# Second mixture layer of a gated model: when the second tile's rows are gathered, and which of ScalarE's and VectorE's work is issued first

## The chip, the cores and the metric

The kernel runs on one core of one Trainium2 chip. TensorE (PE) does the matrix products, ScalarE (ACT) and VectorE (DVE) take results out of PSUM and convert weights, GpSimd (POOL) issues the gathers and scatters of rows, SyncE (SP) issues the loads of weights. The metric is the device time of one execution in microseconds (us), the median of three runs.

## The reference

Attention is followed by two mixture-of-experts layers over 2304 tokens with 512 features and 8 experts of 1024 hidden units. The change lies in the second of them:

```python
def _moe2_ref(x, w_skip, w_gate, w1, w2) -> np.ndarray:
    N, D = x.shape
    E = w_gate.shape[1]
    skip_score = x @ w_skip
    do_compute = skip_score > 0
    out = x.copy()
...
    xc = x[do_compute]
    logits = xc @ w_gate
    e_idx = np.argmax(logits, axis=1)
...
    for e in range(E):
        mask = e_idx == e
        if not mask.any():
            continue
        h = np.maximum(xc[mask] @ w1[e], 0.0)
        y[mask] = gate_w[mask, None] * (h @ w2[e])
    out[do_compute] = xc + y
    return out.astype(np.float32)
```

## The kernel before

The second layer goes through the eight experts one after the other, in places 0 to 7. An expert's tokens are known only when the first layer is done, so they are taken in tiles of 128 rows. The first tile of a place is always computed, by straight code that this document calls region 0 to region 7. A second and a third tile stand behind run-time branches (`tc.If`, L1449 to L1468): `ffn2s` for a second tile of at most 64 rows, `ffn2` for a larger one. In this run place 0 has three tiles, places 2 and 5 a small second one, place 6 a large second one; places 1, 3, 4 and 7 have one tile. Every place issues the gather of a second tile, whether it has rows or not.

A tile goes like this. POOL gathers 128 rows from `out` into a buffer `XB[i]` (`gather2`, L1199). PE transposes them (`xtr2`, L1220, four steps into one PSUM bank), ACT writes the high part (L1224) and DVE the low part (L1225). The product with w1 is 24 matmuls in two halves of 12 (L1243, PSUM banks h0 and h1). ACT takes each half out through a ReLU (L1245, into `oh`), PE transposes it (`htr`, L1254), and ACT and DVE split it (L1260, L1261, `hhh` and `hhl`). The product with w2 is another 24 matmuls (L1278, into `y`): four with the high weights and four with the low ones on the high activations, four on the low activations, for each half. DVE scales and adds the old rows (L1287), POOL scatters the result (L1291).

Each expert's weights are eight pieces of 512 KB. SP loads a piece into one of eight `raw` buffers, ACT rounds it (L960, `wh`), DVE subtracts to get the rest (L962, `wl`), and only then can SP load the next piece into that buffer. A region from 1 to 6 converts eight pieces: the w2 of its own expert and the w1 of the next.

The order on each engine is worked out when the kernel is built. `Plan` collects operations with an estimated length, what they read and write, and a number for precedence (lower goes first among those that are ready), and lays them out in one list per engine. On the chip every engine keeps to its list, so an instruction that waits holds up all that stand behind it on its engine. `KN` holds the numbers: `cpr` for conversions, `r2` for the ReLU, `hc` and `hs` for the split of the hidden values, `x2c` and `x2s` for the split of the transposed rows, `floor` for the time at which POOL counts as free at a region's start. A list `hooks` in the region's code says after which part of a tile the gathers, conversions and transposes are added. `conv()` adds one conversion; `nx` is the buffer (0 or 1) of the next expert's first tile.

Of the kernel before, what the change touches and what calls it, by code (L numbers as in the profile page):

```python
# [10 lines left out]
F32 = mybir.dt.float32  # L11
# [10 lines left out]
N, DM, E, F = 2304, 512, 8, 1024  # L22
# [397 lines left out]
    return dict(kqT=kqT, kq0=kq0, vL=vL, s=s.reshape(NH, S), wgb=wgb)  # L420


KN = dict(hold=0.2, hfrac=0.7, floor=4.3, r2=3, ht=0, hc=2, hs=-1, x2c=2, x2s=3, st=0, r1=1, l1=2, y1=1, y1s=0, o1=1, x1c=2, x1s=2, lgp=-1, mm1=2, tr1=2, g1=0, hv2=(0, 2, 3, 4, 6), lp2=(0, 4, 6), lv1=(1, 3), slm=0, cpr=2, nd=16, sw=0.11, sa=0, sp=0, sa2=0, sp2=1, pp=3, dly=1, x2p=2, x2q=-1, cut=10)


class Plan:
# [346 lines left out]
H4 = NCH // 2  # L773
# [41 lines left out]
def moe(tc, ctx, setup, lw, xs, w1, w2, w9, v1, v2, out, ident):  # L815
# [3 lines left out]
    for _ in gen:  # L819
# [18 lines left out]
    T["io1"] = T["oh"][:, 96:]  # L838
    nc.gpsimd.iota(T["io1"], pattern=[[1, 96], [0, NT]], base=1, channel_multiplier=0,
                   allow_small_or_imprecise_dtypes=True)  # L840
    for t in XB:
        nc.gpsimd.memset(t, 0.0)
    xt = [pool.tile([128, 4, TS], F32R, name="xt" + a) for a in "hl"]
# [43 lines left out]
    def op(eng, dur, r, w, fn, prio=2, **kw):  # L887
        cur["P"].op(eng, dur, fn, r.split(), w.split(), prio, **kw)
# [54 lines left out]
    def conv():  # L943
        n = done["conv"]
        if n >= E * H4 + E * NCH:
            return
        i = n % NW
        j = n % NP if n < E * H4 else (n - E * H4) % NR
        pr = -1 if n < 4 else KN["cpr"]
        w = f"wh{j}a wh{j}b"  # L950
        v = f"wl{j}a wl{j}b"
        if n >= E * H4 and j >= NP:
            w += f" rb{2 * (j - NP)}"
            v += f" rb{2 * (j - NP) + 1}"

        def hi():
            if WH[j] is None:
                WH[j] = pool.tile([128, 1024], F32R, name=f"wh{j}", tag="rb", bufs=2 * (NR - NP))
                WL[j] = pool.tile([128, 1024], F32R, name=f"wl{j}", tag="rb", bufs=2 * (NR - NP))
            return nc.scalar.copy(WH[j], RAW[i])  # L960
        op("ACT", 0.95, f"raw{i}", w + (f" rb{2 * (j - NP) + 1}" if n >= E * H4 and j >= NP else ""), hi, pr)
        op("DVE", 1.13, f"raw{i} wh{j}a wh{j}b", v, lambda: V.tensor_tensor(  # L962
            WL[j], RAW[i], WH[j].bitcast(F32), op=OP.subtract), pr)
        done["conv"] += 1
        dmas()
# [231 lines left out]
    def gather2(i, idx, r):  # L1197
        def g():
            x = nc.gpsimd.indirect_dma_start(out=XB[i][:, :DM], out_offset=None, in_=out[:, :],  # L1199
                                             in_offset=bass.IndirectOffsetOnAxis(ap=idx, axis=0),  # L1200
                                             bounds_check=N - 1, oob_is_err=False)
            nc.gpsimd.memset(spacer, 0.0)  # L1202
            for o in [y for y in scat if y is not None]:
                tc.declare_no_dep(x.ins, o.ins, reason="other rows")
            gat.append(x)
            return x
        op("POOL", 1.1, r, f"xg{i}" + (f" xr{i}" if i < 3 else ""), g, prio=0, xfer=0.73)

    T3 = TR + [rt]
    UK = ["tr0", "tr1", "cnt"]  # L1210
# [86 lines left out]
            return st  # L1297
        op("POOL", 1.1, f"ot{t}", "", sc, xfer=0.73)

    def ffn2s(e, idx, gate):  # L1300
        g, i, s = E + e, 2, 2
        xs2 = yl[:, 0:1024].rearrange("p (k t) -> p k t", k=4)

        def half(f):
            sl = slice(f * 512, f * 512 + 512)
            for k in range(4):
                j = ((g - E) * NCH + k) % NR
                for w in "hl":
                    op("PE", 0.2315, f"zh2 zl2 w{w}{j}{'ab'[f]}", f"h{f}", lambda k=k, j=j, w=w: nc.tensor.matmul(
                        HB[f], xs2[:, k, 0:2 * HS], (WH if w == "h" else WL)[j][:, sl], start=k == 0 and w == "h",  # L1310
                        stop=k == 3 and w == "l"))
            op("ACT", 0.48, f"h{f}", f"ht{f}", lambda: nc.scalar.copy(yt[:, sl], HB[f]), KN["r2"])

        def htr(f):
            b = bank("t3")
            pv = T3[b].rearrange("q (c t) -> q c t", c=4)[:, :, 0:HS]

            def tr():
                for c in range(4):
                    o = f * 512 + c * 128  # L1320
                    x = nc.tensor.matmul(pv[:, c, :], yt[:, o:o + 128], id2, start=True, stop=True)
                return x
            op("PE", 0.86, f"ht{f}", f"{UK[b]}", tr, KN["ht"])
            hk = " ".join(f"hh{k}" for k in range(4 * f, 4 * f + 4))
            lk = " ".join(f"hl{k}" for k in range(4 * f, 4 * f + 4))
            hv, lv = (hh[0][:, 4 * f:4 * f + 4, o:o + HS] for o in (0, HS))
            op("ACT", 0.32, f"{UK[b]}", hk, lambda: nc.scalar.activation(hv, pv, AF.Relu), KN["hc"])
            op("DVE", 0.35, f"{UK[b]} " + hk, lk, lambda: V.scalar_tensor_tensor(
                lv, pv, 0.0, hv.bitcast(F32), op0=OP.max, op1=OP.subtract), KN["hs"])

        half(0)
        half(1)
        htr(0)
        htr(1)
        b = bank("y")
        for k in range(8):
            j = ((g - E) * NCH + 4 + k // 2) % NR
            o = (k % 2) * 512
            for w in "hl":
                op("PE", 0.2315, f"hh{k} hl{k} w{w}{j}{'ab'[k % 2]}", f"yb{b}", lambda k=k, j=j, o=o, w=w: nc.tensor.matmul(  # L1340
                    YB[b], hh[0][:, k, 0:2 * HS], (WH if w == "h" else WL)[j][:, o:o + 512],
                    start=k == 0 and w == "h", stop=k == 7 and w == "l"))
        t = 4 + len(scat) % 2
        scat.append(None)
        me = len(scat) - 1
        op("ACT", 0.48, f"yb{b}", "ht0", lambda: nc.scalar.copy(yt[0:HS, 0:512], YB[b][HS:2 * HS]), KN["r2"])
        op("DVE", 0.66, f"yb{b} ht0", f"ot{t} x1r{t - 3} x1s{t - 3}", lambda: V.tensor_tensor(
            XB[t][:HS, :DM], YB[b][0:HS], yt[0:HS, 0:512], op=OP.add), KN["st"])
        op("DVE", 0.66, f"ot{t} xg{i}", f"ot{t}", lambda: V.scalar_tensor_tensor(
            XB[t][:HS, :DM], XB[t][:HS, :DM], gate[:HS], XB[i][:HS, :DM], op0=OP.mult, op1=OP.add), KN["st"])  # L1350

        def sc():
            st = nc.gpsimd.indirect_dma_start(
                out=out[:, :], out_offset=bass.IndirectOffsetOnAxis(ap=idx[:HS], axis=0), in_=XB[t][:HS, :DM],
                in_offset=None, bounds_check=N - 1, oob_is_err=False)
            nc.gpsimd.memset(spacer, 0.0)
            for o in gat + [x for x in scat if x is not None]:
                tc.declare_no_dep(st.ins, o.ins, reason="other rows")
            scat[me] = st
            return st  # L1360
        op("POOL", 1.1, f"ot{t}", "", sc, xfer=0.4)
# [50 lines left out]
    def col(t, e, j):  # L1412
        return t[:, e, j:j + 1]

    reorder()
    for e in range(E):
        nx = (e + 1) % 2

        def conv2():
            conv()  # L1420
            conv()

        def b0():
            if e + 1 < E:
                gather2(nx, col(tk, e + 1, 0), "tk" + (" " + scs if e == 0 else ""))
            gather2(2, col(tk, e, 1), "tk0 tk")
            conv2()

        def b4():
            xtr2(2, 2)  # L1430

        def b5():
            if e + 1 < E:
                xtr2(nx, nx)
        hooks = [b0, conv2, conv2, conv2, b4, b5]
        if e == 0:
            hooks[2] = hooks[3] = lambda: None
        if e == E - 1:
            hooks[2] = hooks[3] = lambda: None
        if e == 0:  # L1440
            ffn2(0, 0, 0, tks[:, 0:1], Q["er"][:, 1:2], hooks, "er")
        else:
# [6 lines left out]
        rn = nc.values_load(nt[0:1, e:e + 1], min_val=0, max_val=NJ)  # L1449
        with tc.If(rn > 1):  # L1450
            with tc.If(rn < 3):
                ffn2s(e, col(tk, e, 1), tabp[:, 1, e, 1:2])
                cur["P"].emit()
                cur["P"] = Plan()
            with tc.If(rn > 2):  # L1455
                ffn2(e, 2, 2, col(tk, e, 1), tabp[:, 1, e, 1:2], [lambda: gather2(3, col(tk, e, 2), "tk tk0")])
                cur["P"].emit()
                side = cur["P"]
                cur["P"] = Plan()
                with tc.If(rn > 3):  # L1460
                    cur["P"] = Plan(side)
                    xtr2(3, 3)
                    ffn2(e, 3, 3, col(tk, e, 2), tabp[:, 1, e, 2:3])
                    cur["P"].emit()
                    cur["P"] = Plan()
                    with tc.If(rn > NJT + 1):
                        V.memset(jb, 128.0 * NJT)
                        with tc.For_i(NJT + 1, rn, 1):  # L1468
# [14 lines left out]
                            tkj, gtj = T["tkj"], T["gtj"]  # L1483
                            V.tensor_scalar(tkj, rb[:, 0:1], BIG, None, op0=OP.add)
                            V.tensor_reduce(gtj, rb[:, 1:3], axis=AX.X, op=OP.add)
                            gather2(3, tkj[:, 0:1], "tkj")
                            xtr2(3, 2)
                            ffn2(e, 3, 2, tkj[:, 0:1], gtj)
                            cur["P"].emit()
        cur["P"] = Plan(main)  # L1490
        cur["P"].free0["POOL"] = max(cur["P"].free0.get("POOL", 0.0), KN["floor"])

# [45 lines left out]
```

## Time and profile before

| what | value |
|---|---|
| median of 3 runs | 800.18 us (800.17 to 807.49) |
| the profiled execution | 806.63 us |
| its span | 804.9 us |
| PE busy | 702.2 us (87%) |
| DVE busy | 518.2 us (64%) |
| ACT busy | 388.3 us (48%) |
| POOL busy | 263.1 us (33%) |
| regions 1 to 6, from 618.0 us on | 130.2 us together |

PE is the busiest engine. Busy time is an average over attention, the first layer and the second one, and a PE that runs at half its clock counts as busy, so the second layer is read by itself, in windows from one region's first matmul to the next. In the rows below, a time in square brackets is how long the engine sat idle before the instruction, and the name behind the arrow is what it waited for; a q behind an engine's name is its sequencer.

### The profile page before, as it was taken

How to read it: one execution, taken by the hardware profiler on the slowest of the kernel's cores; microseconds unless marked ns; L12 is line 12 of the kernel's file. 1: busy time of each engine (PE TensorE's matmuls, PEld its weight loads, DVE VectorE, ACT ScalarE, POOL GpSimd, SP SyncE). 2: the span in 40 equal slices, each digit the busy share in tenths (PEclk: the TensorE clock that was granted, in tenths of full speed). 3: DMA queues.
4: the chain of work that ended last, by engine and by line, in shares of the span. 5: the costliest groups of instructions: out<-in, count | busy, mean ns of one | idle time of the engine just before them, and what ended most of it. 6: DMA issues, size and time to landing. Idle time of an engine off the chain costs nothing. (4 is left out here: it accounts for less than half of the span.)

```text
span 804.9 us, 13927 instructions
## 1 busy us (share of the span) xinstructions
PE 702.2 (87%) x4539; PEld 589.8 (73%) x4539; DVE 518.2 (64%) x1591; ACT 388.3 (48%) x883; POOL 263.1 (33%) x348
## 2 busy tenths in 40 slices
PE   2889989998995599999999999999989687778696
PEld 1778878887884397978878898888767475556574
DVE  6767879987886757877858754135824456453613
ACT  5858868877881213424324333224614445442512
POOL 7467657665723102212023132201122122220211
PEclk9989999999997699999999999999999789887898
DMA  9999999999911516627427461506911564564300
GB/s 209 206 152 225 227 222 211 239 205 201 225 31 68 192 67 226 226 64 256 182 91 251 153 241 38 165 0 224 371 44 61 195 226 143 174 215 179 126 15 21
DMA packets 58599, 132.16 MB, mean 164 GB/s; under 512 B 27712, under 2 KB 27712, under 8 KB 56576
## 3 DMA queue, kind: packets, MB, share of 16 engines
q1 hardware_dynamic: 30304, 99.30, 40.0%
q0 software_dynamic: 27616, 29.49, 26.1%
q10 hardware_dynamic: 576, 2.10, 0.7%
q8 instruction: 52, 0.85, 0.4%
q14 instruction: 51, 0.42, 0.2%
HBM read 106.62 MB, written 13.76 MB: 150 GB/s over the span
## 5 line engine op out<-in xcount | busy, mean ns | idle before, releaser
L1009 PE MATMUL y<-hf,rb 128*128 128x288 f32 x512 | 137.3, 414 | 0.0
L962 DVE TENSOR_TENSOR wl<-raw,wh 128x1024 fp32r<-128x1024 f32 x96 | 112.6, 1219 | 17.2 <-ACT wh L960 17.1
L960 ACT CAST wh<-raw 128x1024 fp32r<-128x1024 f32 x96 | 95.6, 1045 | 38.6 <-DMA raw<-in_w_dram 22.7
L1009 PEld LDWEIGHTS y<-hf,rb 128*128 128x128 f32 x512 | 92.6, 190 | 21.1
L245 ACT ACTIVATE z<-z,sums 128x576 f32<-128x576 f32 (+2 forms) x144 | 84.7, 588 | 13.9 <-DVE sums L237 12.5
L237 DVE CUSTOM_DVE_ANT_0 z<-s,mask 128x576 f32<-128x576 f32 (+2 forms) x144 | 70.3, 513 | 21.0 <-PE s L226 20.4
L261 PE MATMUL pt<-ident,z 128*128 128x128 f32 (+1 forms) x464 | 80.0, 288 | 1.3 <-DVE ptl L280 0.8
L225 PE MATMUL s<-kq 128*128 128x512 f32 (+2 forms) x192 | 64.7, 344 | 16.6 <-DMA kq<-cneg 14.7
L280 DVE TENSOR_TENSOR ptl<-pt,pth 128x512 fp32r<-128x512 f32 (+2 forms) x128 | 68.2, 551 | 6.0 <-ACT pth L275 5.9
L968 POOL DMA_INDIRECT xb<-xs,k_tok x24 | 32.1, 1339 | 116.6 <-PE y L1009 31.6
L275 ACT CAST pth<-pt 128x512 fp32r<-128x512 f32 (+2 forms) x128 | 60.0, 473 | 18.5 <-PE pt L261 16.9
L1001 ACT ACTIVATE hf<-h 128x288 f32<-128x288 f32 x64 | 26.2, 411 | 77.8 <-PE h L993 70.5
L226 PE MATMUL s<-ka,qa 128*128 128x512 f32 (+2 forms) x192 | 52.6, 328 | 11.3 <-DMA qa<-ql 9.6
L1053 POOL DMA_INDIRECT out_dram<-xb,k_tok x24 | 23.2, 967 | 118.8 <-ACT xb L1036 111.1
L261 PEld LDWEIGHTS pt<-ident,z 128*128 128x128 f32 (+1 forms) x464 | 53.3, 143 | 6.7 <-issue 3.0
L1011 ACT CAST yr<-y 128x288 fp32r<-128x288 f32 x32 | 12.7, 398 | 85.1 <-PE y L1009 81.1
L225 PEld LDWEIGHTS s<-kq 128*128 128x128 f32 x192 | 37.1, 193 | 21.5 <-issue 16.7
L1291 POOL DMA_INDIRECT out_dram<-xb,tk x10 | 10.2, 1015 | 128.7 <-DVE xb L1287 98.3
L289 PE MATMUL y<-pth,vhl 128*128 128x384 f32 (+2 forms) x160 | 51.5, 330 | 0.2 <-ACT yT L306 0.2
L993 PE MATMUL h<-xth,wh 128*128 128x288 f32 x256 | 49.4, 313 | 2.0 <-ACT hf L1001 1.6
L226 PEld LDWEIGHTS s<-ka,qa 128*128 128x128 f32 x192 | 37.0, 195 | 15.9 <-issue 14.0
L289 PE MATMUL y<-ptl,vhl 128*128 128x384 f32 (+2 forms) x160 | 46.9, 322 | 0.0
(328 smaller groups left out, 1636.7 us busy)
## 6 DMA issues: line engine op xcount, KB each, us to landing
raw<-in_v_dram SPq DMA_DIRECT2D x64, 512.0 KB
raw<-in_w_dram SPq DMA_DIRECT2D x32, 512.0 KB
rb<-in_w_dram SPq DMA_DIRECT2D x28, 512.0 KB
raw<-in_kqT_dram SPq DMA_DIRECT2D x15, 576.0 KB
kq<-in_kqT_dram POOLq DMA_DIRECT2D x15, 576.0 KB
vhl<-in_vL_dram POOLq DMA_DIRECT2D x16, 320.0 KB
vraw<-in_vL_dram SPq DMA_DIRECT2D x16, 320.0 KB
xs<-xb SPq DMA_DIRECT2D x16, 288.0 KB
```

The lines of the kernel that those rows point to most:

```text
L225: nc.tensor.matmul(rows[:, o + c0:o + c1], qs_, kb[:, i, c0:c1], start=True, stop=False)
L226: nc.tensor.matmul(rows[:, o + c0:o + c1], ql_, ka[:, i, c0:c1], start=False, stop=True)
L237: nc.vector.tensor_tensor_reduce(z[:, :w], ps[:, o:o + w], mk, op0=OP.add, op1=OP.min, scale=-0.125, scalar=3e38, accum_out=sums[h // 2][: ...
L245: nc.scalar.activation(z[:, :w], z[:, :w], AF.Exp, bias=sm[:, 0:1], scale=-1.0, accum_out=sm[:, 1:2])
L261: nc.tensor.transpose(ps[:jw, k, :], p[:, I0[jb]:I0[jb] + jw], ident)
L275: nc.scalar.copy(hview(PTB[h % 2][0], ib, jbs), ps[:, :len(jbs), :])
L280: nc.vector.tensor_tensor(hview(PTB[h % 2][1], ib, jbs), ps[:, :len(jbs), :], hview(PTB[h % 2][0], ib, jbs).bitcast(F32), op=OP.subtract)
L289: nc.tensor.matmul(y[:, a2 - 192:S - 192], vhl[:, h % G, jb].rearrange("p a d -> p (a d)"), PTB[h % 2][t][:, jb, a2 - 192:], start=n_ == 0 ...
L960: return nc.scalar.copy(WH[j], RAW[i])
L962: op("DVE", 1.13, f"raw{i} wh{j}a wh{j}b", v, lambda: V.tensor_tensor(WL[j], RAW[i], WH[j].bitcast(F32), op=OP.subtract), pr)
L993: x = nc.tensor.matmul(ps, a[(p * H4 + k) % NP][:, m * 128:(m + 1) * 128], xt[c][:, k, :], start=k == 0 and i == 0, stop=k == 3 and i == 2)
L1009: op("PE", 0.49, f"rb{r} hf{k}", f"yb{b}", lambda r=r, o=o, k=k: nc.tensor.matmul(ps, RB[r][:, o:o + 128], hf[:, k, :], start=k == 0, stop ...
```

## The change

The rows of a second tile are gathered one place ahead, into `XB[2]` or `XB[3]` by turns; a new buffer (`xb6`) takes the third tile's rows. They are transposed at the start of their region. The next expert's first tile is transposed in the middle of the region, where the order puts it, and no longer at its end. In the order, the ReLU, the split of the hidden values on ACT and the split of the transposed rows get lower numbers (`r2` 3 to -1, `hc` 2 to -1, `x2c` 2 to 0, `x2s` 3 to 0), and the second layer's conversions a higher one (`cp2` 4 in the place of `cpr` 2). POOL no longer counts as taken for the first 4.3 us of a region.

```diff
-KN = dict(hold=0.2, hfrac=0.7, floor=4.3, r2=3, ht=0, hc=2, hs=-1, x2c=2, x2s=3, st=0, ...
+KN = dict(hold=0.2, hfrac=0.7, cp2=4, r2=-1, ht=0, hc=-1, hs=-1, x2c=0, x2s=0, st=0, ...
...
+    XB.append(pool.tile([128, DM], F32, name="xb6"))
     for t in XB:
         nc.gpsimd.memset(t, 0.0)
...
-        pr = -1 if n < 4 else KN["cpr"]
+        pr = -1 if n < 4 else KN["cpr"] if n < E * H4 else KN["cp2"]
...
+        i2, n2 = 2 + e % 2, 2 + nx
+
         def b0():
+            if e == 0:
+                gather2(2, col(tk, 0, 1), "tk0 tk " + scs)
             if e + 1 < E:
                 gather2(nx, col(tk, e + 1, 0), "tk" + (" " + scs if e == 0 else ""))
-            gather2(2, col(tk, e, 1), "tk0 tk")
             conv2()
-
-        def b4():
-            xtr2(2, 2)
-
-        def b5():
+            if e + 1 < E:
+                gather2(n2, col(tk, e + 1, 1), "tk0 tk")
+
+        def b1():
+            conv2()
+            xtr2(i2, 2)
+
+        def b3():
+            conv2()
             if e + 1 < E:
                 xtr2(nx, nx)
-        hooks = [b0, conv2, conv2, conv2, b4, b5]
+        hooks = [b0, b1, conv2, b3]
         if e == 0:
-            hooks[2] = hooks[3] = lambda: None
+            hooks = [b0, conv2, lambda: xtr2(i2, 2), lambda: xtr2(nx, nx)]
         if e == E - 1:
-            hooks[2] = hooks[3] = lambda: None
+            hooks = [b0, b1]
...
         cur["P"] = Plan(main)
-        cur["P"].free0["POOL"] = max(cur["P"].free0.get("POOL", 0.0), KN["floor"])
```

In the lists of the change the lines from L843 on stand 1 to 8 numbers higher than before (L1220 is L1221 there, L1245 is L1246, L1260 is L1261). The first place is ACT in region 4, before: the last six of the eight conversions, the two ReLUs (`oh`), the two splits (`hhh`), and the splits of the second tile's rows (`yl`) and of the next first tile's (`xth`).

```order
L960 CAST wh_3490<-raw_3479 128x1024
L960 CAST wh_3491<-raw_3480 128x1024
L960 CAST wh_3492<-raw_3473 128x1024
L960 CAST wh_3493<-raw_3474 128x1024
L960 CAST wh_3494<-raw_3475 128x1024
L960 CAST wh_3495<-raw_3476 128x1024
L1245 ACTIVATE oh<-h_3538 128x512
L1245 ACTIVATE oh<-h_3539 128x512
L1260 CAST hhh<-tr_3542 128x512
L1260 CAST hhh<-tr_3543 128x512
L1224 CAST yl<-rt 128x512
L1224 CAST xth<-tr_3542 128x4x128
```

The same engine and region in the change, from the region's second instruction on.

```order
L1225 CAST yl<-tr_3544 128x512
L961 CAST wh_3489<-raw_3478 128x1024
L961 CAST wh_3490<-raw_3479 128x1024
L1246 ACTIVATE oh<-h_3540 128x512
L961 CAST wh_3491<-raw_3480 128x1024
L1261 CAST hhh<-tr_3545 128x512
L961 CAST wh_3492<-raw_3473 128x1024
L1246 ACTIVATE oh<-h_3541 128x512
L961 CAST wh_3493<-raw_3474 128x1024
L1261 CAST hhh<-rt 128x512
L961 CAST wh_3494<-raw_3475 128x1024
L1225 CAST xth<-tr_3544 128x4x128
```

All eight conversions stood ahead of the first ReLU; now three do, and the others stand between the evacuations. The second place is PE in region 4, before, from the last w1 matmul on: the two transposes of the hidden tile, one matmul of w2, the transpose of the second tile's rows (`rt` from `xb_3514`), and the rest of w2.

```order
L1243 MATMUL h_3539<-wh_6856,xtl 128x512
L1254 MATMUL tr_3542<-ident,oh 128x128 x4
L1254 MATMUL tr_3543<-ident,oh 128x128 x4
L1278 MATMUL y_3540<-wh_3488,hhh 128x512
L1220 MATMUL rt<-ident,xb_3514 128x128 x4
L1278 MATMUL y_3540<-wh_3488,hhh 128x512
L1278 MATMUL y_3540<-wh_3489,hhh 128x512 x2
```

PE in the same region of the change, from the last w1 matmul on. The second tile's rows (`xb_3514`) have been transposed ahead of the first w1 matmul.

```order
L1244 MATMUL h_3541<-wh_6858,xtl 128x512
L1279 MATMUL y_3542<-wh_3488,hhh 128x512 x2
L1279 MATMUL y_3542<-wh_3489,hhh 128x512 x2
L1279 MATMUL y_3542<-wl_3496,hhh 128x512
L1255 MATMUL rt<-ident,oh 128x128 x4
L1279 MATMUL y_3542<-wl_3496,hhh 128x512
L1279 MATMUL y_3542<-wl_3497,hhh 128x512 x2
L1279 MATMUL y_3542<-wh_3488,hhl 128x512
L1221 MATMUL tr_3544<-ident,xb_3513 128x128 x4
L1279 MATMUL y_3542<-wh_3488,hhl 128x512
```

The transpose that stood behind one w2 matmul is gone from here, and the next expert's first tile (`xb_3513`), which was transposed behind the last w2 matmul, now comes behind the ninth. In region 1 it stands ahead of the first w2 matmul, as these rows of PE in the change show, from the last w1 matmul on.

```order
L1244 MATMUL h_3541<-wh_6858,xtl 128x512
L1221 MATMUL tr_3544<-ident,xb_3512 128x128 x4
L1279 MATMUL y_3543<-wh_3488,hhh 128x512 x2
L1279 MATMUL y_3543<-wh_3489,hhh 128x512 x2
L1255 MATMUL rt<-ident,oh 128x128 x4
```

From region to region this place moves back: in regions 1 to 6 it has 0, 3, 5, 9, 14 and 18 of the 24 matmuls of w2 ahead of it.

## Rows read from the trace of the kernel before

**Rows 1.** Windows, regions 1 to 6, then 7: length, busy (x), PEclk, DMA, GB/s.
```profile
618.00:640.60 22.60, 17.08 (x64) 13.11 (x64) 12.27 (x14) 10.80 (x14) 4.86 (x6) 0.77 0.58 207
640.60:661.40 20.80, 16.72 (x64) 13.07 (x65) 12.07 (x13) 10.45 (x13) 4.65 (x6) 0.84 0.63 224
673.00:695.60 22.60, 17.93 (x64) 13.70 (x64) 12.47 (x14) 10.86 (x14) 4.81 (x7) 0.77 0.55 198
695.60:717.10 21.50, 15.79 (x64) 12.03 (x64) 12.47 (x14) 10.98 (x14) 4.74 (x7) 0.84 0.62 219
717.10:738.60 21.50, 17.16 (x63) 13.46 (x64) 11.76 (x13) 10.45 (x13) 4.51 (x6) 0.76 0.61 217
750.20:771.40 21.20, 15.93 (x65) 12.14 (x65) 12.41 (x14) 10.88 (x14) 4.47 (x7) 0.84 0.36 119
784.40:797.10 12.70, 12.62 (x60) 9.93 (x59) 6.64 (x8) 6.16 (x9) 2.31 (x4) 1.00 0.05 15
```

**Rows 2.** Timeline of PE, region 7: one hidden transpose and the next matmul.
```profile
789.12 0.60 PE L1254 MATMUL tr<-ident,oh 128*128 128x128 f32 x4
789.48 0.47 PE L1243 MATMUL h<-wh,xtl 128*128 128x512 f32 x1
```

**Rows 3.** Waits of PE, 618 to 784 us: total, times, longest.
```profile
PE tr L1220 <- DMA xb<-out_dram,tk: 8.7, 4, 2.9
PE tr L1254 <- ACT oh L1245: 7.8, 5, 2.5
PE rt L1220 <- DMA xb<-out_dram,tk: 4.9, 2, 2.7
...
PE rt L1254 <- ACT oh L1245: 2.5, 1, 2.5
PE h L1243 <- issue: 1.8, 1, 1.8
```

**Rows 4.** Timeline of PE, region 4: start, length, instruction, idle time before it.
```profile
695.62 0.50 PE L1243 MATMUL h<-wh,xth 128*128 128x512 f32 x1 [0.87 <-ACTq L1450]
...
701.07 0.40 PE L1243 MATMUL h<-wh,xtl 128*128 128x512 f32 x1
703.92 1.14 PE L1254 MATMUL tr<-ident,oh 128*128 128x128 f32 x8 [2.45 <-ACT oh L1245]
705.25 0.80 PE L1278 MATMUL y<-wh,hhh 128*128 128x512 f32 x1 [0.19 <-ACT hhh L1260]
708.26 1.08 PE L1220 MATMUL rt<-ident,xb 128*128 128x128 f32 x4 [2.22 <-DMA xb<-out_dram,tk]
```

**Rows 5.** Timelines of ACT and DVE, region 4.
```profile
695.69 7.68 ACT L960 CAST wh<-raw 128x1024 fp32r<-128x1024 f32 x8 [0.32 <-ACTq L1450]
703.28 1.07 ACT L1245 ACTIVATE oh<-h 128x512 f32<-128x512 f32 x2
...
696.77 9.18 DVE L962 TENSOR_TENSOR wl<-raw,wh 128x1024 fp32r<-128x1024 f32 x8 [0.68 <-ACT wh L960]
```

**Rows 6.** The window of region 4 in which the clock was halved.
```profile
705.00:711.80 6.80, 4.39 (x13) 3.27 (x13) 2.84 (x4) 1.35 (x3) 0.00 (x0) 0.50 0.98 392
```

**Rows 7.** Timelines: POOL's gathers in region 4 and region 0; PE's wait there.
```profile
698.48 1.55 POOL L1199 DMA_INDIRECT xb<-out_dram,tk  x1 [1.99 <-DVE wl L962]
...
586.10 1.02 POOL L1199 DMA_INDIRECT xb<-out_dram,tk  x1 [0.21 <-issue]
...
588.24 0.66 PE L1220 MATMUL tr<-ident,xb 128*128 128x128 f32 x4 [0.45 <-DMA xb<-out_dram,tk]
```

**Rows 8.** DMA queue of gathers, 702 to 705.3 us: packets, MB, share.
```profile
q0 software_dynamic: 79, 0.26, 26.3%
```

**Rows 9.** POOL clears the buffers; its next wait (source of L842, timeline).
```profile
L842 POOL MEMSET xb<- x6: 567/571/584, 258.8 to 261.4; 128x576 f32 x6
...
272.83 1.08 POOL L968 DMA_INDIRECT xb<-xs,k_tok  x1 [10.60 <-DVE r_v L595]
```

**Rows 10.** DMA queue of gathers, 626 to 628 us, region 1.
```profile
q0 software_dynamic: 80, 0.26, 36.5%
```

More of the change, by code (lines that the diff above doesn't have):

```diff
@@ L420, in host_layout @@
     return dict(kqT=kqT, kq0=kq0, vL=vL, s=s.reshape(NH, S), wgb=wgb)
-KN = dict(hold=0.2, hfrac=0.7, floor=4.3, r2=3, ht=0, hc=2, hs=-1, x2c=2, x2s=3, st=0, r1=1, l1=2, y1=1, y1s=0, o1=1, x1c=2, x1s=2, lgp=-1, mm1=2, tr1=2, g1=0, hv2=(0, 2, 3, 4, 6), lp2=(0, 4, 6), lv1=(1, 3), slm=0, cpr=2, nd=16, sw=0.11, sa=0, sp=0, sa2=0, sp2=1, pp=3, dly=1, x2p=2, x2q=-1, cut=10)
+KN = dict(hold=0.2, hfrac=0.7, cp2=4, r2=-1, ht=0, hc=-1, hs=-1, x2c=0, x2s=0, st=0, r1=1, l1=2, y1=1, y1s=0, o1=1, x1c=2, x1s=2, lgp=-1, mm1=2, tr1=2, g1=0, hv2=(0, 2, 3, 4, 6), lp2=(0, 4, 6), lv1=(1, 3), slm=0, cpr=2, nd=16, sw=0.11, sa=0, sp=0, sa2=0, sp2=1, pp=3, dly=1, x2p=2, x2q=-1, cut=10)
 class Plan:
@@ L1206, in g @@
             return x
-        op("POOL", 1.1, r, f"xg{i}" + (f" xr{i}" if i < 3 else ""), g, prio=0, xfer=0.73)
+        op("POOL", 1.1, r, f"xg{i}" + (f" xr{i}" if i < 3 else " x1r0 x1s0" if i == 3 else ""), g, prio=0, xfer=0.73)
     T3 = TR + [rt]
@@ L1298, in ffn2, with ffn2s @@
         op("POOL", 1.1, f"ot{t}", "", sc, xfer=0.73)
-    def ffn2s(e, idx, gate):
-        g, i, s = E + e, 2, 2
+    def ffn2s(e, i, idx, gate):
+        g, s = E + e, 2
         xs2 = yl[:, 0:1024].rearrange("p (k t) -> p k t", k=4)
@@ L1451, in moe @@
             with tc.If(rn < 3):
-                ffn2s(e, col(tk, e, 1), tabp[:, 1, e, 1:2])
+                ffn2s(e, i2, col(tk, e, 1), tabp[:, 1, e, 1:2])
                 cur["P"].emit()
@@ L1461, in moe @@
                     cur["P"] = Plan(side)
-                    xtr2(3, 3)
-                    ffn2(e, 3, 3, col(tk, e, 2), tabp[:, 1, e, 2:3])
+                    xtr2(6, 3)
+                    ffn2(e, 6, 3, col(tk, e, 2), tabp[:, 1, e, 2:3])
                     cur["P"].emit()
@@ L1485, in moe @@
                             V.tensor_reduce(gtj, rb[:, 1:3], axis=AX.X, op=OP.add)
-                            gather2(3, tkj[:, 0:1], "tkj")
-                            xtr2(3, 2)
-                            ffn2(e, 3, 2, tkj[:, 0:1], gtj)
+                            gather2(6, tkj[:, 0:1], "tkj")
+                            xtr2(6, 2)
+                            ffn2(e, 6, 2, tkj[:, 0:1], gtj)
                             cur["P"].emit()
         cur["P"] = Plan(main)
-        cur["P"].free0["POOL"] = max(cur["P"].free0.get("POOL", 0.0), KN["floor"])
 def host_moe(moe_w1, moe_w2, moe2_w_gate, moe2_w_skip, moe2_w1, moe2_w2):
```

2 lines of the change are left out of this document (1 added, 1 removed).

## The prediction

> **What bounds the kernel now.** I first cut the second layer into windows, one from each region's first matmul to the next region or to the second tile's branch [rows 1]. Regions 1 to 6 last 22.6, 20.8, 22.6, 21.5, 21.5 and 21.2 us, 130.2 together, and PE is busy for 100.6 of them. Region 7 does the same 48 matmuls in 12.70 us, with PE busy for 12.62 at a granted clock of 1.00; it has one step of row transposes less and converts four pieces of weights where the others convert eight. A step of four transposes takes 0.36 us (789.12 to 789.48) [rows 2], so a tile is 12.98 us of PE work at the full clock, six are 77.9, and 52.3 us of the 130.2 are something else. The reader should see two parts in them: 130.2 - 100.6 = 29.6 us in which PE is idle, and 100.6 - 77.9 = 22.7 us by which its busy time is too long.
>
> Next I asked what PE waited for between 618 and 784 us [rows 3]. It waited 7.8 + 2.5 = 10.3 us for ACT's ReLU, once in each of the six regions, 8.7 + 4.9 = 13.6 us for the gather in front of a row transpose, also once in each, and 1.8 us at one place for nothing that the profile shows. The other 3.9 us are starts of regions and small waits.
>
> Region 4, which no branch touches on either side, shows how this comes about. Its 24 matmuls on w1 run from 695.62 to 701.07, 5.45 us for 23 steps, so 0.237 us each; then PE is idle for 2.45 us until the ReLU [rows 4], because ACT goes through eight conversions from 695.69 on, 7.68 us or 0.96 each, and starts the ReLU at 703.28 [rows 5]. One w2 matmul later PE is idle for another 2.22 us, until the second tile's rows are in the buffer, at 708.26 [rows 4]. This tile has no rows in places 1, 3 and 4, and PE waits for it all the same. From 705.0 to 711.8 the granted clock is 0.50, the lower of the two levels (1.2 in place of 2.4 GHz) [rows 6]; before it fell PE had been idle for 2.45 us. All six regions have a mean clock of 0.76 to 0.84, and region 7, where PE never waits for long, has 1.00 [rows 1]. So the 22.7 us too many are the half clock, and they follow from the idle time: 22.7 / 29.6 = 0.77 us for each idle one.
>
> **The change part by part.** *The ReLU ahead of the conversions.* In regions 2 to 6 three conversions and one split (about 0.6) stand ahead of the first ReLU: 3 x 0.96 + 0.6 = 3.5 us after the region's start. The first half of w1 is done after 0.36 + 12 x 0.237 = 3.2 us, so the ReLU runs until about 4.1. PE comes to the hidden transpose behind 17 matmuls, at 0.36 + 17 x 0.237 = 4.4: no wait. The second ReLU has two conversions and a split more ahead of it, 6.6 to 7.2 us; PE needs it at 0.36 + 24 x 0.237 + 0.36 + 5 x 0.237 = 7.6 in regions 3 to 6. I keep 0.4 us per region for what such sums miss, 2.4 in place of 10.3 (bounds 0 and 10.3).
>
> *What the conversions lose.* They are the cover for this, so they must not become late. DVE is busy for 11.8 to 12.5 us in a region [rows 1] and starts its first subtraction 1.15 us after PE (696.77 and 695.62) [rows 4, 5]; it needs about 13.5 us, and a region will last longer than that by the sum below. The loads need 219 GB/s x 21.5 us = 4.7 MB per region [rows 1], 12.0 us at the 392 GB/s that the chip moved in the half-clock window [rows 6]. Neither becomes the bound; I cost them at nothing, and the second rival says what they cost otherwise.
>
> *The second tile's rows one place ahead.* The number of gathers, transposes and scatters stays the same, and so does POOL's row of two gathers and a scatter per region; region 0 issues a third gather that is needed a region later, and region 7 none. The rows now have a whole region to land, so the 13.6 us of waiting at this transpose go, and region 0 saves its 0.45 [rows 7].
>
> *The next first tile in the middle.* This is the new wait. Its gather used to be needed at the region's end; now its transpose has 0, 3, 5, 9, 14 and 18 matmuls of w2 ahead of it in regions 1 to 6, and PE holds everything behind it. With one row transpose, 24 matmuls, and one hidden transpose (two from region 3 on) before it, PE is there after 6.4, 7.1, 7.95, 8.9, 10.1 and 11.0 us. When does the gather land? In region 4 it is issued at 698.48 [rows 7], 2.9 us after PE's start, and its 0.26 MB have passed by 705.3 [rows 8], 9.7 us after the start. The bounds are far apart: in region 0, with no weight loads beside it, a gather was used 2.14 us after its issue (586.10 to 588.24) [rows 7], which would be 5.0; the second gather of region 4 was there after 12.6 (708.26) [rows 4]. I take 9.7, the row of this very gather; the loads beside it will come no denser than now, and PE starts some tenths earlier, which about cancel. The waits are then 3.3, 2.6, 1.75, 0.8, 0 and 0: 8.45 us, in regions 1 to 4 only.
>
> A gather's issue took 1.02 us in region 0, where DVE was idle, and 1.55 in region 4 beside the subtractions of weights [rows 5, 7]. The Trainium skill (SBUF — State Buffer, Who interferes with whom) has it that a VectorE instruction with two SBUF inputs gets in the way of GpSimd's reads but, as it infers, not of the writing of descriptors. By that the issue would take 1.0 here too, the landing would be 0.5 earlier, and the change would give some 3 us more; the trace speaks against it, and the sum goes by the trace.
>
> *The clock.* 0.77 x (8.45 + 1.8), the new waits and the unexplained one: 7.9 us at the half clock in place of 22.7.
>
> *The rest.* The 1.8 us stay (bounds 0 and 1.8). At a region's start PE waited for ACT's split of the next tile (0.87 in region 4) [rows 4], which is now done earlier; the branch itself stays. I take 2.4 of the 3.9 (bounds 0 and 3.9). The seventh buffer costs POOL one more clearing of at most 0.57 us, ahead of a wait of 10.60 us [rows 9]: nothing.
>
> **The sum.** Regions 1 to 6 become 77.9 + 2.4 + 8.45 + 7.9 + 1.8 + 2.4 = 100.9 us, 29.3 less than 130.2, and with region 0 29.8 less. The profiled execution took 806.63 us, of which the span is 804.9; it would take 776.8. It lies 6.45 above the median of 800.18, and I take the saving over unchanged: 770.4 us.
>
> **The rivals.** *The first gather lands early.* If it lands after 5 to 8 us, as the one without loads beside it suggests, the waits shrink to nothing in most regions: at 5.0 the sum is 77.9 + 2.4 + 1.4 + 1.8 + 2.4 = 85.9, which gives 755. Against it: the loads start as early as before.
>
> *The conversions come late.* They now stand behind the evacuations, and in regions 2 and 3 the last ones stand behind the split of a tile that waits for the gather. If each region starts 1 us before its first weights are ready, that is 6 us and 0.77 x 6 at the half clock, 10.6 in all: 781. For it: DVE is busy for 12 us of a region that shrinks to 14 in the last places. Against it: the sum leaves at least half a us.
>
> *The first gather becomes the bound, and the kernel slower.* PE now stops for it early in a region where nothing else is ready. With a landing after 11 us the waits are 4.6, 3.9, 3.05, 2.1, 0.9 and 0, and the sum gives 781; after 12.6 us, the second gather's landing, they are 24.2 in all, the half clock 20.0, and the sum is 128.6, which gives 798. From about 13 us on the change costs more than it gives: at 14 us the waits are 32.6 and the half clock 26.4, so 13 us more than before, 813. For it: the gather passes through the same DMA engines as 4 MB of weights. Against it: none of its landings seen is later than 10 us (626 to 628 in region 1, PE's start at 618.0) [rows 1, 10]. The Trainium skill (DMA: Bandwidth & Descriptors, Queues, rings and completion order) says that each DMA engine takes turns between the queues, a packet at a time, so that a gather would not stand behind all the loads; region 4, where it passed beside them, agrees.
>
> *The change does not do what it says*: the ReLU still waits, because ACT now waits for the weights or for PE in between. Then the waits only change their names, about 800. In region 4 ACT's eight conversions ran without a gap [rows 5], so the weights were there.
>
> **How the numbers follow.** The forecast, a landing between 8 and 11 us, has 0.68 and reaches from 760 to 781. An early landing has 0.14 (755 to 760), late conversions 0.06 (up to 784), a landing after 11 to 13 us 0.07 (781 to 800), slower 0.02, no effect 0.03. The range of 757 to 782 leaves out about 0.17. A measurement of this kernel can tell 1% (8 us) from no change: faster than 792 in the first three and most of the fourth, 0.93; within 1% 0.05; slower 0.02.
>
> **What would show it.** In the profile after, ACT's ReLU should start about 3.5 us after a region's start and PE's wait for it should be gone; PE's wait for a gather should stand in regions 1 to 4 alone, growing smaller from one to the next; the mean clock of regions 5 and 6 should be near 1.00, their length near 14 us, and that of region 1 near 19. I would be wrong if the first gather's landing moves by more than 2 us, or if PE waits for `wl` or `raw` in regions 3 to 5, where no second tile gives the loads time.

## The result and the profile after

The changed kernel took 776.7 us, the median of four runs (774.5 to 780.2), beside 801.1 for the kernel before: ratio 0.968, 95% interval 0.962 to 0.975. The forecast of 770.4 lay 6 us below, and its range of 757 to 782 holds the time. The profiled execution has a span of 772.8 us, 32.1 less than before. Not all of that is the change: layer 2 (from the gather of place 0's first tile, at 553.8 us before and 547.5 after, to the end) shrank from 251.1 to 225.3 us, by 25.8; the other 6.3 us lie ahead of it, where nothing was changed.

Windows of the changed kernel, regions 1 to 6 and 7, with the columns of [rows 1]:

```profile
615.80:633.40 17.60, 13.21 (x64) 10.45 (x65) 12.60 (x13) 10.94 (x15) 5.71 (x8) 1.00 0.75 250
633.40:650.90 17.50, 14.92 (x64) 12.18 (x65) 11.72 (x12) 10.95 (x14) 3.18 (x4) 0.80 0.63 211
663.00:680.00 17.00, 14.58 (x64) 11.68 (x64) 12.59 (x13) 10.46 (x15) 4.53 (x8) 0.90 0.76 240
680.00:698.00 18.00, 14.54 (x64) 11.66 (x65) 12.49 (x13) 11.08 (x15) 3.99 (x6) 0.91 0.82 280
698.00:712.50 14.50, 14.49 (x65) 11.92 (x66) 11.66 (x12) 11.05 (x14) 2.20 (x4) 0.88 0.77 255
724.50:739.50 15.00, 14.64 (x65) 11.68 (x65) 12.19 (x13) 10.42 (x14) 3.22 (x6) 0.89 0.51 158
753.00:765.70 12.70, 12.02 (x58) 9.38 (x56) 7.33 (x8) 5.82 (x8) 0.86 (x2) 1.00 0.05 15
```

Regions 1 to 6 last 99.6 us (100.9 forecast, 130.2 before). PE is busy for 86.4 of them and idle for 13.2. The waits of PE from 615 us on, as in [rows 3], show that the idle time has other names than forecast:

```profile
PE rt L1221 <- PEq L1458: 6.5, 2, 3.4
PE tr L1221 <- DVEq L1463: 4.6, 2, 2.3
PE rt L1221 <- issue: 2.6, 1, 2.6
PE tr L1221 <- issue: 2.5, 1, 2.5
PE tr L1221 <- DMA xb<-out_dram,tk: 1.2, 1, 1.2
```

The waits for ReLU and for the second tile's rows are gone. One wait for the next first tile is left, 1.24 us in region 1. Nearly all the rest, 3.12 + 2.56, 2.46 and 3.40 = 11.5 us, stands at the starts of regions 2, 4 and 5, right behind the branch over the code of tiles that places 1, 3 and 4 do not have. PE around the first of these starts:

```profile
629.23 1.07 PE L1279 MATMUL y<-wh,hhl 128*128 128x512 f32 x4
633.42 0.41 PE L1221 MATMUL rt<-ident,xb 128*128 128x128 f32 x1 [3.12 <-PEq L1458]
636.38 0.90 PE L1221 MATMUL rt<-ident,xb 128*128 128x128 f32 x3 [2.56 <-issue]
```

The branch instruction itself on PE's sequencer (count: shortest/median/longest in ns, first and last start), after, at the ends of regions 1, 3 and 4:

```profile
L1458 PEldq COMPARE_BRANCH  x1: 4819/4819/4819, 628.3 to 628.3; - x1
...
L1458 PEldq COMPARE_BRANCH  x1: 4537/4537/4537, 675.2 to 675.2; - x1
...
L1458 PEldq COMPARE_BRANCH  x1: 5494/5494/5494, 692.2 to 692.2; - x1
```

The same three before:

```profile
L1450 PEldq COMPARE_BRANCH  x1: 3844/3844/3844, 636.0 to 636.0; - x1
...
L1450 PEldq COMPARE_BRANCH  x1: 3388/3388/3388, 691.0 to 691.0; - x1
...
L1450 PEldq COMPARE_BRANCH  x1: 3608/3608/3608, 712.9 to 712.9; - x1
```

The long branches were there before, unseen. The sequencer reaches the branch while PE still has products queued. The first branch of before began at 636.0, and PE had work until 639.94, as the end of region 1 shows:

```profile
639.34 0.60 PE L1220 MATMUL tr<-ident,xb 128*128 128x128 f32 x4
640.65 0.49 PE L1243 MATMUL h<-wh,xth 128*128 128x512 f32 x1 [0.72 <-ACTq L1450]
642.94 0.50 PE L1243 MATMUL h<-wl,xth 128*128 128x512 f32 x1 [1.79 <-issue]
```

So 3.9 us of work covered a branch of 3.84 (3.75 and 3.4 at the other two places). After the change 2.0, 2.4 and 2.4 us of work stand against 4.8, 4.5 and 5.5. Two things have changed, then: the cover fell by 4.2 us over the three places, and the branches grew by 4.0. Why the queue was longer before is argued, not shown: a PE that stops for ReLU and gathers lets its sequencer get ahead. The other runs below fit this: when the branch begins, PE has 16, 17 and 16 matmuls left before and 13 to 16 in the runs that keep waits for ReLU (e2, e8, e11), but 8 to 14 in those that do not (e1 and the changed kernel).

The traces also show what a long branch waits for. In all 61 branches of PE of over 1 us in layer 2 of the fourteen traces, a packet of 16 KB on queue q8, a queue of instructions, lands 1.3 to 1.5 us before the branch ends. In the shortest ones (3.3 us) it starts 0.9 to 1.0 us after the branch does, in the three branches of before 1.0 to 1.5, and in the three of the changed kernel 2.2 to 3.2. So the branches grew because their packet started later. The packet of the first one after (DMA queues, 630 to 632 us), beside the weights on q1:

```profile
q1 hardware_dynamic: 152, 0.54, 91.6%
q8 instruction: 1, 0.02, 3.0%
```

### The profile page after: what moved, and what is told of

It reads as the page before. It is cut to its first block, busy times and chain, and to the rows that moved or that the text cites. A ratio compares the mean times of both kernels' runs of the same rounds, so it can differ in the third digit from the quotient of the medians.

```text
span 772.8 us, 13881 instructions
## 1 busy us (share of the span) xinstructions
PE 687.8 (89%) x4538; PEld 579.2 (75%) x4539; DVE 518.1 (67%) x1591; ACT 389.1 (50%) x883; POOL 258.9 (33%) x349
## 5 line engine op out<-in xcount | busy, mean ns | idle before, releaser
L963 DVE TENSOR_TENSOR wl<-raw,wh 128x1024 fp32r<-128x1024 f32 x96 | 115.3, 1219 | 35.5 <-ACT wh L961 35.4
L961 ACT CAST wh<-raw 128x1024 fp32r<-128x1024 f32 x96 | 98.8, 1047 | 48.9 <-DMA raw<-in_w_dram 24.3
L245 ACT ACTIVATE z<-z,sums 128x576 f32<-128x576 f32 (+2 forms) x144 | 84.7, 589 | 12.0 <-DVE sums L237 10.3
L136 POOL TENSOR_TENSOR ql<-raw,kq 64x576 fp32r<-64x576 f32 x30 | 42.5, 1418 | 11.5 <-DMA kq<-in_kqT_dram 5.5
L994 PE MATMUL h<-xth,wl 128*128 128x288 f32 x256 | 46.4, 300 | 0.0
```

The costliest lines, as they stand in the source:

```text
L245: nc.scalar.activation(z[:, :w], z[:, :w], AF.Exp, bias=sm[:, 0:1], scale=-1.0, accum_out=sm[:, 1:2])
L994: x = nc.tensor.matmul(ps, a[(p * H4 + k) % NP][:, m * 128:(m + 1) * 128], xt[c][:, k, :], start=k == 0 and i == 0, stop=k == 3 and i == 2)
```

## The experiments

My theory was that the change gains by taking away both waits, each by its own part, and pays some of it back at the branch. Rivals: one part does it all; the new wait at the regions' starts is for a gather or a conversion and only stands beside the branch.

### Which part gains

The precedence alone, and the gather ahead alone:

```diff
 # e1: the kernel before, with
+cp2=4, r2=-1, hc=-1, x2c=0, x2s=0   (and cp2 for the conversions of layer 2)
 # e2: the changed kernel, with
+cp2=2, r2=3, hc=2, x2c=2, x2s=3
```

> The precedence of evacuations alone; the gathers, their buffers and the pieces between the products stay as before. Theory (the two parts take away two waits that stand in a row, and the second ends at a landing that does not come earlier): the 2.45 us waits for ReLU go, but the row transposes of the second tile then wait longer for the same gather, so a region keeps most of its 21.7 us; total 792 to 800 us, ratio 0.99 to 1.00. Rival (the precedence is what made the kernel faster): ratio 0.968 to 0.975, 776 to 781 us.

> The gather one expert ahead alone, with the old precedence numbers (conversions ahead of ReLU). Theory: the waits for the second tile's gather go, the waits for ReLU of about 2.4 us per region stay and with them a part of the half clock; 3 us of six regions gained, ratio 0.975 to 0.985 (781 to 789 us). Rival (the gather-ahead is what made the kernel faster): ratio 0.968 or below. Rival (precedence is): ratio 0.99 to 1.00.

Measured: e1 0.969 (0.962 to 0.976), e2 0.978 (0.971 to 0.984). e2 came as the theory had it, with the waits for ReLU still there (6.8 + 1.0 us) and none for a second tile's rows. For e1 the rival was right and my theory wrong: the precedence alone gives, on balance, all that the change gives. Layer 2 lasts 224.5 us in e1's trace, beside 225.3 in the changed kernel. The waits for the second tile's rows are nearly gone in e1, though nothing gathers them earlier. PE in region 4 of e1, which starts at 674.9:

```profile
685.80 0.60 PE L1220 MATMUL tr<-ident,xb 128*128 128x128 f32 x4
686.31 1.20 PE L1278 MATMUL y<-wh,hhh 128*128 128x512 f32 x4
687.35 0.86 PE L1278 MATMUL y<-wl,hhh 128*128 128x512 f32 x3
688.05 0.60 PE L1220 MATMUL rt<-ident,xb 128*128 128x128 f32 x4
...
691.66 0.47 PE L1243 MATMUL h<-wh,xth 128*128 128x512 f32 x1 [1.85 <-PEq L1450]
```

The row transposes now stand behind 12 and 19 products of w2, not behind one [rows 4]: the plan, in which the ReLU is early, has products ready to put ahead of them. Two runs with one number each take this apart, e8 (`r2` alone) and e11 (`floor` alone, which moves nothing but the transposes):

```diff
 # e8: the kernel before, with
-r2=3
+r2=-1
 # e11: the kernel before, with
-floor=4.3
+floor=7.3
```

> One number of the precedence alone: the ReLU goes ahead of the conversions, the evacuations of the transposes stay where they were. Theory (the planner, which now sees an early ReLU, also puts the row transposes of the second tile some twelve products later): both waits go and most of the gain is there, ratio 0.970 to 0.980. Rival (the other evacuations count as much, being behind conversions on DVE and ACT): ratio 0.985 to 0.995.

> The kernel before with one number of the planner changed: it takes POOL to be free at 7.3 instead of 4.3 us into a region, and so puts the row transposes of the second tile some sixteen products later; the precedence and the gathers stay. Theory (the 2.2 us wait for the gather of the second tile comes from where the transposes stand, not from when the gather is started): these waits go from regions 1 to 6, the waits for ReLU stay, ratio 0.980 to 0.988. Rival (the gather's landing sets the end of the region wherever the transposes stand): within 0.5% of the kernel before.

Measured: e8 0.972 (0.968 to 0.977), as its theory had it, and e11 0.977 (0.972 to 0.981), a little more than its theory gave. In e8 the transposes stand behind 11 products, ten products of 0.23 us later than before, and waits for the gather are left over in four of the regions. Waits of PE in e8, regions 1 to 6:

```profile
PE h L1243 <- PEq L1450: 5.1, 3, 2.4
PE rt L1220 <- DMA xb<-out_dram,tk: 4.7, 2, 2.5
PE tr L1220 <- DMA xb<-out_dram,tk: 3.9, 3, 2.6
...
PE tr L1254 <- ACT oh L1245: 3.3, 4, 1.0
```

In e11, with the transposes behind 20 products in most regions, no wait for a gather is left, and those for ReLU are as before (7.7 + 2.4, beside 10.3 in [rows 3]):

```profile
PE tr L1254 <- ACT oh L1245: 7.7, 5, 2.4
PE h L1243 <- PEq L1450: 6.2, 3, 2.9
PE h L1243 <- PEq L1455: 3.6, 2, 1.8
PE h L1243 <- issue: 3.0, 1, 3.0
PE rt L1254 <- ACT oh L1245: 2.4, 1, 2.4
```

So the 13.6 us of waiting for the second tile's rows came from the place of the transposes, and one number that gathers nothing earlier takes them away. The gains don't add (e8 moves the transposes as well): 2.8% and 2.3% alone, 3.1% with the whole precedence. What is left over shows at the branch. PE's idle time at the starts of regions 2, 4 and 5 is 4.3 us before (0.72, 1.79, 0.87, 0.88), 8.1 in e8, 9.3 in e11, 9.9 in e1 (2.15 of it put down to DVE's `wl`) and 11.5 in the changed kernel.

### What the wait behind the branch is

e3 leaves out the conditional code at the places 1, 3, 4 and 7, e4 only what is behind the small second tile there, e10 the third tile and the loop at all places but 0; e5 loads an eighth of each weight piece in layer 2, so that it computes with other weights but takes the same branches.

```diff
 # e3
+        if e in (1, 3, 4, 7):
+            cur["P"] = Plan(main)
+            continue
         rn = nc.values_load(nt[0:1, e:e + 1], min_val=0, max_val=NJ)
 # e10, ahead of the third tile (e4 likewise, ahead of the large second one at those places); the gather of a third tile's rows goes too
+                if e > 0:
+                    cur["P"] = Plan(main)
+                    continue
                 with tc.If(rn > 3):
 # e5
-                    dst, src[ds(reg[p], 1), k % 4]...
+                    dst[:, 0:128], src[ds(reg[p], 1), k % 4, :, 0:128]...
```

> The changed kernel without the conditional code at the places 1, 3, 4 and 7, whose experts have one tile in this data (what is left out is the code for more rows there). Theory (the wait at the start of regions 2, 4 and 5 is for instructions behind a branch over code that is not taken): the idle times 3.12 and 2.56, 2.46, 3.40 us, 11.5 in all, go, and 3.4 us at half clock in each of the three regions run in 1.7; 14 to 17 us less than the changed kernel, 760 to 763 us, ratio 0.948 to 0.952. Rival (these waits are for the gather of the second tile or for a conversion that is late, and the branch lies beside them): the same waits stand there, 773 to 777 us, ratio 0.965 to 0.970.

> The changed kernel with only the small second tile behind the branch of the places 1, 3, 4 and 7 (the code for over 192 rows is left out there). It tells whether the length of what is jumped over matters. If the price is that of a target that has not been loaded yet, and 64 matmuls are near enough: the branch of PE shrinks from 4.5 to 5.5 us to under 1 us and the time is that without branches, ratio 0.948 to 0.953. If every branch that is taken over code costs its own loading: branches of 3.4 to 5.5 us as in the changed kernel, ratio 0.966 to 0.970.

> The changed kernel with the code for a third tile and for more rows only at place 0 (left out at the places 1 to 7; this data needs it at place 0 alone). What the branch jumps over falls from four blocks of products to two. If distance decides and two blocks are near enough: branches under 1 us at the places 1, 3, 4 and 7, ratio 0.957 to 0.962, as with the small tile alone. If two blocks are too far: branches of 3.4 to 5.5 us as in the changed kernel, ratio 0.966 to 0.970.

> The changed kernel with weight loads of layer 2 cut from 512 KB to 64 KB each (the other seven eighths of a piece keep what lay there, so layer 2 computes with other weights; the routing, and with it every branch, is the same). If the weight loads lengthen the branches over code that is not taken: the 4.54 to 5.49 us of PE's branches at the places 1, 3 and 4 shrink to about the 3.4 us of those at the places 2, 5 and 7, the idle times at the starts of regions 2, 4 and 5 (11.5 us) fall to 6 to 8 us, and the time is 4 to 6 us below the changed kernel. If the branch costs what it costs by its own loading: branches and idle times as they are, and the time within 2 us of the changed kernel.

e3: 0.955 (0.949 to 0.961), a little above the theory's 0.948 to 0.952, which the interval reaches, and clear of the rival's 0.965 to 0.970. The waits at the three starts are gone; in their place a wait of 3.2 us for the gather stands in region 2. So they were the branch's, and not those of a late conversion. e4: 0.960 (0.954 to 0.966), a little above what was expected of near code; e10: 0.954 (0.949 to 0.959), a little below it. In both the branch is there and runs, and is short; e10, end of region 1:

```profile
L1458 PEldq COMPARE_BRANCH  x1: 327/327/327, 629.4 to 629.4; - x1
```

It is the distance that costs. Counted in the program, with a product's weight load as an instruction of its own, the branch jumps over some 95 of PE's instructions in e4, 200 in e10 and 500 in the changed kernel. No packet of q8 passes during e10's three short branches. Of the idle time at the three starts 3.1 us are left in e10, ended by DVE's sequencer. e10 has another gain, which e4 has not: the jump behind a second tile that was computed (L1463) takes 0.35 us at most, where it took 3.37. And with the branches short, the wait that I had forecast stands there. Waits of PE in e10:

```profile
PE tr L1221 <- DMA xb<-out_dram,tk: 5.4, 4, 1.9
PE rt L1221 <- DMA xb<-out_dram,tk: 3.0, 1, 3.0
```

These are 1.24, 2.99, 1.90 and 1.36 us in regions 1 to 4, 7.5 together, and 0.9 in region 6. In the changed kernel the stop behind the branch moves PE back against POOL's gather: in region 2 the gather is issued 2.5 us ahead of PE's first product (634.45 and 636.94), in e10 2.4 behind it; in region 4 it is 1.3 us behind it, in e10 2.7. What was to be a wait in the middle of the region is paid at its start.

e5 (one run, 761.8 us): the three branches take 3.82, 3.68 and 3.34 us where they took 4.82, 4.54 and 5.49, and the idle time at the starts is 8.0 us in place of 11.5. So weight loads that run at a region's end lengthen the branch, by 0.9 to 2.2 us, and 3.3 us or more are left (one execution of each kernel): the packet on q8 starts after 1.0 to 1.5 us again. Layer 2 is 11.4 us shorter, twice what I expected: in the regions the clock is at half only once, for 6.8 us in region 2, beside 20.5 us in five stretches in the changed kernel, and that is worth another 7 us.

### What the branch cost before, and the gather ahead without it

e9 is the kernel before and e7 is e1, both without the conditional code at the places 1, 3, 4 and 7 (the edit of e3).

> The kernel before, without the conditional code at the places 1, 3, 4 and 7 (the code for more rows is left out there). Theory (before the change the branch ran while PE still had some 3.9 us of products queued, so it cost little): only the short idle times at the starts of regions 2, 4 and 5 go (0.72 and 1.79, 0.87, 0.88 us), 2 to 5 us less with their clock, ratio 0.994 to 0.998. Rival (the branch costs the same in any kernel, 15.7 us by the change in the changed kernel): ratio 0.978 to 0.984.

> The precedence alone, and no conditional code at the places 1, 3, 4 and 7 (the code for more rows is left out there). It tells what the gather one expert ahead is worth where no branch stops PE. Theory (the wait behind the branch covers the two gathers, which start while PE stands still): without the branch waits for gathers come up in their place, of 1.5 to 3 us in regions 2, 4 and 5, and the kernel is 4 to 8 us slower than the changed kernel without these branches (ratio 0.9551): ratio 0.960 to 0.966. Rival (the gather ahead is worth nothing under the new precedence): ratio 0.950 to 0.956, the 4 us of region 0 included.

Measured: e9 0.991 (0.988 to 0.994), 7 us, between what the theory and the rival gave. The saving is not the one that the theory named. PE's idle time at the three starts was small before and falls from 4.3 to 2.0 us, but the waits for gathers fall from 13.6 to 7.9: those of regions 2, 4 and 5 are gone, where POOL now issues the gather 1.3 us after PE's first product and no longer 2.9 to 3.0; those of regions 1, 3 and 6, ahead of which a branch has stayed, are still there. POOL's gather in region 2, before:

```profile
643.63 1.44 POOL L1199 DMA_INDIRECT xb<-out_dram,tk  x1 [1.90 <-DVE wl L962]
```

PE's first product and POOL's gather in e9:

```profile
637.13 0.50 PE L1243 MATMUL h<-wh,xth 128*128 128x512 f32 x1 [0.68 <-ACT xth L1224]
...
638.47 1.72 POOL L1199 DMA_INDIRECT xb<-out_dram,tk  x1 [0.23 <-issue]
```

So the branch was mostly covered for PE, and still had a price, by way of POOL. In the one trace of each kernel layer 2 is 12.4 us shorter in e9 (238.7 beside 251.1), more than the interval of the times allows, so the size is open.

e7: 0.950 (0.946 to 0.954). Without branches the precedence is worth 0.991 - 0.950 = 4.1% of the time before, with them 3.1%. The difference, 8 us, has an interval almost as wide as itself, and by layer 2 of the traces it is 1 us (27.8 and 26.6). That the idle time behind the branches grew is shown; how much of the gain went into them is not. Against e3 (0.955) e7 is no slower, and by layer 2 of the traces (210.9 and 211.3 us) the two are the same. So the rival was right once more: the gather one place ahead is worth nothing on balance beside the new precedence, with or without branches. Yet it is not worth nothing everywhere. From place 1's first product to the end the changed kernel takes 156.5 us beside 161.2 in e1, and e3 142.6 beside 147.5 in e7: 4.7 and 4.9 us gained, which place 0 gives back.

### Place 0

The layer's start and place 0's three tiles take longer wherever the rows are gathered ahead: from the layer's start to place 1's first product 68.8 us after and 64.3 before, 63.3 in e1. e6 puts region 0's row transposes back to where they were:

```diff
-            hooks = [b0, conv2, lambda: xtr2(i2, 2), lambda: xtr2(nx, nx)]
+            hooks = [b0, conv2, lambda: None, lambda: None, lambda: xtr2(i2, 2), lambda: xtr2(nx, nx)]
```

> The changed kernel with the two groups of row transposes of region 0 back in their old places (within and behind the second products). Theory: region 0 gets back its waits of 0.82 and 0.68 us and its full clock, 3 to 4 us; 771 to 774 us, ratio 0.962 to 0.966. Rival (the half clock of region 0 comes from the wait behind its branch, which stays): within 1 us of the changed kernel, ratio 0.968.

Measured: 0.967 (0.963 to 0.970), not to be told from the changed kernel; the same stretch is 67.5 us in its trace. Two waits for gathers (0.68 and 0.64) are still there.

The 4.5 us can be read from the traces. About 1 us is idle time of PE (6.9 us in the stretch, beside 5.9 before). The rest is the clock: 6.8 us at half of it, at the start of place 0's second tile, which is worth some 3.4. Windows after, then before at the same point:

```profile
585.70:592.50 6.80, 5.91 (x14) 4.67 (x15) 0.37 (x1) 0.35 (x1) 1.10 (x2) 0.50 0.10 27
...
591.90:598.70 6.80, 6.72 (x31) 5.63 (x32) 0.69 (x1) 1.55 (x3) 1.53 (x4) 1.00 0.20 65
```

Where it begins PE stops three times within 5 us, for 0.82, 0.68 (both for gathers) and 1.86; before it stops there for 0.45 and 1.48. All seven runs that gather ahead (the changed kernel, e2, e3, e4, e5, e6, e10) have 3.4 or 6.8 us of half clock at this point, and none of the others has.

### A version that is faster than both

e12 takes the precedence alone and leaves nothing out. Behind place 0 one branch looks at the largest number of tiles of the other places; code with the two kinds of second tile comes first, a copy with everything behind it.

```diff
+    big = nc.values_load(nm[0:1, 0:1], min_val=0, max_val=NJ)
+    with tc.If(big < 4):
+        for e in range(1, E):
+            place(e, False)
...
+    with tc.If(big > 3):
+        cur["P"] = after(main)
+        for e in range(1, E):
+            place(e, True)
```

> A version that leaves nothing out: the precedence alone (old gathers), and behind place 0 one branch on the largest number of tiles of the other places. If none needs a third tile, the places 1 to 7 run in code that holds only the two kinds of second tile; a full copy, with the third tile and the loop, stands behind it and is jumped over once, at the end of the program. Theory (the price lies in jumping over too much code, place by place): the branches at the places 1, 3 and 4 fall under 1 us, the time is that of the precedence without branches (ratio 0.950) plus up to 3 us for one more branch behind place 0 and the jump at the end: ratio 0.950 to 0.957. Rival (the jump at the end, or the larger program, costs what the short jumps gain): ratio 0.962 to 0.970.

Measured: 767.8 us, 0.956 (0.952 to 0.961): as the theory had it, and below the interval of the changed kernel (0.962 to 0.975). Windows of regions 2, 4 and 5 of e12:

```profile
635.50:650.20 14.70, 13.02 (x64) 10.65 (x64) 13.34 (x14) 11.14 (x14) 5.11 (x8) 1.00 0.78 271
...
676.30:690.40 14.10, 13.66 (x64) 10.28 (x64) 12.24 (x14) 10.93 (x14) 4.75 (x6) 1.00 0.87 314
690.40:705.90 15.50, 13.25 (x64) 10.64 (x64) 13.48 (x15) 11.22 (x14) 4.84 (x8) 1.00 0.91 328
```

They last 44.3 us where the changed kernel has 50.0, at a clock of 1.00. The one long jump is left, over the copy, at the end of the program:

```profile
L1518 PEldq COMPARE_BRANCH  x1: 3742/3742/3742, 758.3 to 758.3; - x1
```

## Why the prediction was right, and which of its steps were not

The sum for regions 1 to 6 was 77.9 us of products and 23.0 of other things; measured were 77.9 and 21.7 (13.2 idle, and 86.4 - 77.9 = 8.5 at the half clock). The total of the regions held because two steps were off against each other: the waits for the next first tile came out 7.2 us lower than forecast, those at the branches 7.3 us higher (11.5 beside 1.8 + 2.4). That the one goes when the other comes is shown by e10; that they are of one size is luck. The 6 us by which the whole time missed are mostly place 0's.

*The ReLU ahead of the conversions*: right. No wait for ReLU is left, where 2.4 us were kept. ACT in region 4 starts the first one 5.05 us after PE (680.08), not the 3.5 that was to show it, because it waits for the products, which run at half the clock from 681.3 to 684.7, and no longer for conversions:

```profile
681.36 1.99 ACT L961 CAST wh<-raw 128x1024 fp32r<-128x1024 f32 x2
685.13 0.60 ACT L1246 ACTIVATE oh<-h 128x512 f32<-128x512 f32 x1 [1.78 <-PE h L1244]
```

*The conversions cost nothing*: right. No wait for `wl` or `raw` shows in regions 1 to 6.

*The second tile's rows one place ahead*: the waits went as forecast, but the step gives the wrong reason. "The rows now have a whole region to land, so the 13.6 us of waiting at this transpose go": e11 takes them away with the old gathers, and e1 all but 2.8 us of them. I had read "waits for the gather" as "the gather is late"; the row said as well that the transposes stood too early, behind one product. The rivals named no case in which one half of the change does all.

*The next first tile in the middle*: 8.45 us forecast, 1.24 measured in region 1 and none behind it. The landing was not far off: in e10, which has 7.5 us of these waits in the same four regions, they end 10.3 to 10.5 us after PE's start in regions 2 to 4, where 9.7 was forecast. The step fell with the next one.

*The rest, "the branch itself stays"*: this is the step that failed. It stayed, but it grew and its cover went. 2.4 us for starts of regions and 1.8 for the unexplained "issue" became 11.5 us at three starts. I had called region 4 one "which no branch touches on either side"; PE's sequencer spends 3.39 us in a branch ahead of it and 3.61 behind it. The 1.8 us of "issue" in [rows 3] and waits of 0.7 to 0.9 us were all that was to be seen of three branches of 3.4 to 3.8 us, and I took what was seen for the whole. Here the Trainium skill (Runtime: NRT & Kernel Launch, Instruction fetch mechanics) has the rule that I left out: a taken branch whose target lies outside the stretch of program already fetched has to wait for a DMA that brings it in. The trace agrees, in the packet on q8 that each long branch waits for, in e4, e10 and e12 (0.32 to 0.36 us over some 95 and 200 instructions) against the changed kernel (4.5 to 5.5 over 500), and in e5, where the branch is faster with fewer weights on the same DMA engines.

*The clock*: 0.77 us per idle one forecast; 8.5 / 13.2 = 0.64 measured, 8.5 us where 7.9 were forecast. It did not come back where it was to: regions 5 and 6 have 0.88 and 0.89, not 1.00.

*Region 0*: 0.45 us saved in the forecast; the stretch up to place 1 lost 4.5, three quarters of it at the half clock, a term that the forecast had for regions 1 to 6 alone.

## What to carry to other kernels

In these runs a branch over code that is not taken was cheap for PE where its target was near or PE had work queued for longer than the jump, and even then it delayed another engine's gather. A change that takes waits away can take that cover too, so look up how long each branch runs, not only how long the engine was seen to wait for it. Code that data rarely needs is better put behind one jump outside the loop than behind one in each turn (e12). And before a transfer is started earlier, try to put its first reader later: one number in the order (e11) did here as much as two buffers and moved gathers (e2), and a pair of edits should be costed with each half alone.

## What the runs showed of the hardware that was not expected

PE's jump over some 500 instructions took 3.4 to 5.5 us in the changed kernel and 0.33 over 200 in e10. Behind some long jumps comes a second stop, after the first instruction at the target: 1.79 us before, 2.56 in the changed kernel, 3.0 in e5, always at region 2; that it is the next piece of the program being fetched is argued from packets of the instruction queues in this time, not shown. A gather's issue on POOL took 2.00 us in region 2 of the changed kernel beside DVE's subtraction of weights (634.45) and 1.00 right after it, with DVE idle (636.76). In no trace did one in places 0 to 7 take over 1.1 us without such a subtraction beside it, but some took 1.0 beside one (1.01 at 698.88).
